# A small triangular solve on VectorE, and decays stored without their padding, in a recurrence kernel

## The chip, the cores and the metric

The kernel runs on one core of a Trainium2 chip. The metric is the device time of one execution in microseconds (us). Executions of one kernel scatter: eleven runs of the kernel before took 1129.26 to 1141.66 us in one set of rounds and 1132.16 to 1147.00 us in another. A kernel is always timed next to runs of the kernel before on the same chip, and compared with those; a ratio counts runs of the undisturbed (fast) state alone. In the profiles PE is TensorE, PEld its weight loads, DVE VectorE, ACT ScalarE, POOL GpSimd and SP SyncE; the granted clock is the share of TensorE's full clock that it was given.

## The reference

A recurrence over 768 time steps for 4 batches and 8 heads of 40 values, then a feed-forward layer over the 3,072 tokens:

```python
for t in range(S):                                   # S = 768; state: [B, H, 40, 40]
    y[:, :, t] = einsum('bhd,bhde->bhe', rt, state)
    Sa = einsum('bhde,bhe->bhd', state, at)
    state = state * wt[:, :, None, :] - einsum('bhd,bhe->bhde', Sa, bt)
    state = state + einsum('bhd,bhe->bhde', vt, kt)
x = y as [B*S, H*D]                                  # 3072 x 320
out = maximum(x @ w_in, 0)**2 @ w_out                # 320 -> 2048 -> 320
```

The kernel works on chunks of 128 steps: 24 chunks (6 in time for each of 4 batches, batch running fastest), so that the recurrence becomes matrix products and a triangular system per chunk and head. `rest` makes a chunk's products with k, v and r, `chain` carries the state through it, and the feed-forward layer is woven in once groups of chunks are done.

## The kernel before

Three parts matter. First, the preparation of a chunk (`early`): products of decays by scans, their reciprocals, and a' = a times decay, all in one tile `dec` of 128 partitions with 3 x 4 x 130 values. Heads sit in pairs: one in partitions 0 to 39, the other in 64 to 103; the rest is padding. For all chunks but the first two the tile is stored to DRAM and read back an iteration ahead of its use:

```python
    def load(i, g=None):
        x_ = loaded[i] = {"k": fetch("k", k, i)}
        if g is not None:
            g["dec"] = new("dec", [128, 3, NP, C + 2], 2)
            nc.sync.dma_start(out=g["dec"], in_=kept_e[i])
        x_["r"] = fetch("r", r, i)
        ...
    def early(i, g=None):
        dec = decays.next() if g is None else new("dec", [128, 3, NP, C + 2], 2)
        if g is not None:
            nc.vector.memset(dec[:, :A_, :, MID:MID + 1], 1.0)
        ...                      # scans, reciprocals, bT, a' on VectorE
        if g is None:
            store(kept_e[i], dec)
        ...                      # N = products of a' and bT, stored to kept_q or kept_d
```

Second, the triangular solve. N of one or more chunks (a "unit"; the first two units are one chunk each) is gathered from DRAM into `half_n`, solved by pairs of small operations on GpSimd, stored, and read back as `blocks`, from which T, the inverse, is joined:

```python
    def solve(u, between={}):
        ...
        for s in range(size - 1):
            if s in between:
                between[s]()
            ...
            nc.gpsimd.tensor_tensor(p_, part[...], t3[...], Alu.mult)
            nc.gpsimd.tensor_tensor(t3[:, :n, s + 1:], t3[:, :n, s + 1:], p_, Alu.subtract)
        nc.gpsimd.dma_start(out=to, in_=ts)
    def inverses(i, g, queue=nc.sync):
        blocks = new("blocks", [128, H, Q], 1)
        for col in range(classes(u)):
            queue.dma_start(out=blocks[col::classes(u)], in_=...)
        ...                      # transpose on VectorE, small products, T
```

Third, the order at the start. The program gives each engine a stream of operations in its own order; `go` advances a generator by a step. While GpSimd solves unit 0, VectorE prepares chunks 2 and 3 (`e2`, `e3`):

```python
    solve(0, {12: lambda: take(1, own)})      # take: fetch the next unit's N
    go(r0)
    load_early(3)
    go(r0, 4)
    go(e2, 2)
    load(1)
    go(first_slot)
    ...                                       # e2 and e3 to their ends
    join = inverses(0, ready[0])
    go(join)
    go(e3)
    flush()
    solve(1, {8: lambda: weights_by(0, nc.gpsimd), 20: lambda: take(2, own)})
    run(r0)
    run(join)
    weights_by(1, nc.sync)                    # 1 MB of weights on the SP queue
```

## Time and profile before

| | before |
|---|---|
| median of 3 runs (range) | 1133.54 us (1133.11 to 1136.49) |
| span of the profiled run, mean granted clock | 1135.1 us, 0.908 |
| first product with T on TensorE | 59.06 us |
| chunk 0's tokens on VectorE | 95.81 us |
| chunk 3's tokens | 226.55 us |
| last chunk's tokens | 1057.83 us |

The last four rows are the milestones. "Tokens" is the product of VectorE that ends a chunk. Each is read from one profiled run, so a few us can be chance: the kernel `fill_only` below ends 5.7 us late in its profile, taken in the slowest of its six runs, and has a ratio of 1.0008. In the timeline of the kernel before (start, duration, engine, line, operation, output and inputs, and in brackets the idle time ahead of it and what ended that) they are:

```profile
95.81 0.63 DVE L615 TENSOR_TENSOR tokens<-ps_c,dec 128x512 f32<-128x512 f32 x1
...
226.55 0.69 DVE L615 TENSOR_TENSOR tokens<-ps_c,dec 128x512 f32<-128x512 f32 x1 [3.04 <-PE ps_c L87]
...
1057.83 0.69 DVE L615 TENSOR_TENSOR tokens<-ps_c,dec 128x512 f32<-128x512 f32 x1 [1.96 <-PE ps_c L87]
```

The list of waits (engine, line and output that waited, what it waited for, us in total, times, longest) has four kinds of inputs for the kernel before, 13.0 us together:

```profile
PE ps_w L315 <- DMA in_w<-in_w_dram: 4.9, 2, 4.3
PE ps_w L315 <- DMA in_r<-in_r_dram: 4.3, 3, 2.7
PE ps_w L315 <- DMA in_v<-in_v_dram: 2.6, 2, 2.1
...
PE ps_w L315 <- DMA in_k<-in_k_dram: 1.2, 1, 1.2
```

### The profile page before, as it was taken

What the parts mean: (1) busy time and instruction counts of PE and PEld (TensorE: products, weight loads), DVE (VectorE), ACT (ScalarE), POOL (GpSimd) and SP (SyncE); (2) the same over time, 40 slices, a digit from 0 to 9 for tenths busy, and PEclk for the clock granted to TensorE, in tenths of its full rate; (3) what the DMA queues carried; (4) which work ended last, traced back from release to release, by engine and by line L of the source; (5) the groups of instructions that cost most, each with busy time, mean ns of one, the idle gap of its engine ahead of it and who ended that gap; (6) DMA issues with size and microseconds to landing.
All of it is one profiled execution on the core that took longest, in us unless ns stands there. A gap on an engine that the chain in (4) does not pass through costs nothing.

```text
span 1135.1 us, 19336 instructions
## 1 busy us (share of the span) xinstructions
PE 1029.9 (91%) x7632; PEld 811.9 (72%) x7632; DVE 482.1 (42%) x1004; ACT 246.2 (22%) x547; POOL 651.7 (57%) x1129
## 2 busy tenths in 40 slices
PE   6385787799999999999999999999999999999998
PEld 5375676668777777777777777777777777777666
DVE  6367877727355155154264253353143133330211
ACT  2123233222221122122112122113021121221111
POOL 5886628877874999603999802999858810000000
PEclk8666656689999999999989999999998999999999
DMA  9889977583648505519515518414243342030000
GB/s 116 154 151 210 182 177 178 124 154 77 135 106 156 121 36 109 152 39 167 116 48 101 123 65 150 118 49 84 58 117 69 77 90 58 10 83 12 7 12 12
DMA packets 262370, 113.48 MB, mean 100 GB/s; under 512 B 244168, under 2 KB 250440, under 8 KB 260616
## 3 DMA queue, kind: packets, MB, share of 16 engines
q1 hardware_dynamic: 257944, 93.24, 40.2%
q0 software_dynamic: 3248, 18.88, 7.0%
q8 instruction: 60, 0.98, 0.4%
q10 hardware_dynamic: 1088, 0.13, 0.2%
q14 instruction: 30, 0.25, 0.1%
HBM read 75.77 MB, written 34.48 MB: 97 GB/s over the span
## 4 chain that ended last, share of the span: by engine, by line
PE 69%; DVE 11%; DMA 10%; SPq 3%; POOL 2%; issue 2%; ACT 2%; DVEq 0%; POOLq 0%; ACTq 0%
PE ps_f L87 34%; PE ps_c L87 19%; PE ps_w L87 11%; PE ps_w L315 3%; DMA in_v<-in_v_dram 3%; DVE decay L358 1%; DVE decay L359 1%; PE ps_w L533 1%; SPq L108 1%; DMA in_r<-in_r_dram 1%; DMA blocks<-kept_t 1%; POOL half_t L435 1%; POOL half_p L433 1%; DMA in_w<-in_w_dram 1%; PE ps_c L543 1%
## 5 line engine op out<-in xcount | busy, mean ns | idle before, releaser
L433 POOL TENSOR_TENSOR half_p<-half_n,half_t 128x70 f32<-128x70 f32 (+52 forms) x502 | 288.5, 575 | 104.9 <-DMA half_n<-kept_d 55.4
L435 POOL TENSOR_TENSOR half_t<-half_t,half_p 128x70 f32<-128x70 f32 (+52 forms) x502 | 315.2, 628 | 39.3
L643 DVE TENSOR_TENSOR hid<-ps_f,hid 128x256 f32<-128x256 f32 x176 | 73.9, 420 | 350.3 <-ACT hid L642 349.9
L87 PE MATMUL ps_f<-w_out,hid 128*128 128x320 f32 x704 | 208.2, 444 | 0.1
L87 PE MATMUL ps_f<-tokens,w_in 128*128 128x256 f32 x704 | 199.5, 410 | 0.0
L87 PEld LDWEIGHTS ps_f<-w_out,hid 128*128 128x128 f32 x704 | 130.4, 193 | 49.5 <-issue 2.4
L87 PEld LDWEIGHTS ps_f<-tokens,w_in 128*128 128x128 f32 x704 | 124.6, 196 | 43.5 <-issue 30.3
L642 ACT ACTIVATE hid<-ps_f 128x256 f32<-128x256 f32 x176 | 67.4, 383 | 269.1 <-PE ps_f L87 268.6
L87 PE MATMUL ps_f<-tokens,w_third 64*128 64x256 f32 x352 | 86.0, 425 | 8.1 <-DVE hid L643 6.0
L87 PEld LDWEIGHTS ps_c<-xr,T 64*64 64x64 f32 x768 | 54.9, 150 | 23.6 <-issue 13.8
L87 PE MATMUL ps_c<-xr,T 64*64 64x40 f32 x768 | 60.7, 241 | 7.2 <-DMA T<-kept_t 2.4
L410 POOL DMA_DIRECT2D half_n<-kept_d x18 | 8.9, 501 | 98.0 <-DMA kept_d<-N 92.9
L87 PEld LDWEIGHTS ps_f<-tokens,w_third 64*128 64x128 f32 x352 | 40.0, 190 | 34.9 <-DVE hid L643 23.0
L354 DVE TENSOR_TENSOR_SCAN decay<-ps_w,ones 128x64 f32<-128x64 f32 x88 | 23.6, 268 | 85.1 <-PE ps_w L315 85.1
L87 PEld LDWEIGHTS ps_c<-in_v,A 128*128 128x128 f32 x384 | 51.2, 209 | 2.3
L87 PE MATMUL ps_c<-in_v,A 128*128 128x40 f32 x384 | 50.2, 294 | 0.0
L87 PE MATMUL ps_w<-rT,xnT 40*128 40x128 f32 x384 | 36.4, 309 | 12.6 <-DVE RV L331 12.1
L87 PEld LDWEIGHTS ps_w<-rT,xnT 40*128 40x128 f32 x384 | 29.9, 206 | 22.9 <-DVE RV L331 18.9
L615 DVE TENSOR_TENSOR tokens<-ps_c,dec 128x512 f32<-128x512 f32 x24 | 16.5, 688 | 66.1 <-PE ps_c L87 66.1
L545 ACT COPY sd<-ps_c 128x512 f32<-128x512 f32 x20 | 11.7, 586 | 144.8 <-PE ps_c L543 144.8
L87 PE MATMUL ps_w<-decay,bT 40*128 40x128 f32 x352 | 28.4, 307 | 14.6 <-DVE decay L363 14.6
L370 ACT COPY N<-ps_w 128x512 f32<-128x512 f32 x48 | 25.8, 589 | 63.8 <-PE ps_w L87 44.2
(148 smaller groups left out, 1441.8 us busy)
## 6 DMA issues: line engine op xcount, KB each, us to landing
kept_e<-decay SPq DMA_DIRECT2D x22, 780.0 KB
dec<-kept_e SPq DMA_DIRECT2D x22, 780.0 KB
half_n<-kept_d POOLq DMA_DIRECT2D x12, 384.0 KB, 9.4
half_n<-kept_d POOLq DMA_DIRECT2D x6, 768.0 KB, 11.5
in_w<-in_w_dram SPq DMA_DIRECT2D x24, 160.0 KB
in_ab<-in_b_dram SPq DMA_DIRECT2D x24, 160.0 KB
in_ab<-in_a_dram SPq DMA_DIRECT2D x24, 160.0 KB
in_k<-in_k_dram SPq DMA_DIRECT2D x24, 160.0 KB
```

The source lines that it names most:

```text
L87: nc.tensor.matmul(o, l_, r_, start=start, stop=True, skip_group_check=True)
L108: later(lambda: queue.dma_start(out=out_, in_=in_), steps)
L315: nc.tensor.transpose(p_[:, q * 128:(q + 1) * 128], pair(x_, q), ident)
L354: nc.vector.tensor_tensor_scan(up[:, q, MID + 1:C + 1], wT[:, q, MID:], ones, 1.0, Alu.mult, Alu.mult)
L358: nc.vector.reciprocal(down[:, :, MID + 1:C + 1], up[:, :, MID + 1:C + 1])
L370: nc.scalar.copy(t_[:, e * NP:(e + 1) * NP], p_)
L433: nc.gpsimd.tensor_tensor(p_, part[:, at:at + m_].unsqueeze(1).to_broadcast([128, n, m_]), t3[:, :n, s:s + 1].to_broadcast([128, n, m_]), ...
L435: nc.gpsimd.tensor_tensor(t3[:, :n, s + 1:], t3[:, :n, s + 1:], p_, Alu.subtract)
L545: nc.scalar.copy(sd.rearrange("p q e d -> p q (e d)"), quads(p_))
L615: nc.vector.tensor_tensor(t_, y_, g["up"][:, :, :C], Alu.mult)
L642: nc.scalar.activation(h_, p_, Act.Relu)
L643: nc.vector.tensor_tensor(h_, p_, h_, Alu.mult)
```

## The change

The intent has two parts. GpSimd's solve of the first unit is on the way to the first T, and VectorE was expected to do it faster; so this one solve goes to VectorE, with its input issued ahead and its products in PSUM, and its result goes to DRAM and back on ScalarE's queue. And the decays go without their padding: two transfers of 40 rows (243.75 KB each) instead of one of 128 (780 KB), for which the tiles must hold valid padding, so GpSimd fills them once at the start. The diff, cut to its core:

```diff
@@ load
-            g["dec"] = new("dec", [128, 3, NP, C + 2], 2)
-            nc.sync.dma_start(out=g["dec"], in_=kept_e[i])
+            g["dec"] = whole_decays.next()
+            for e, rows in enumerate(both):
+                nc.sync.dma_start(out=g["dec"][rows], in_=kept_e[i][e])
@@ rings
+    whole_decays = Ring("whole", 2, [128, 3, NP, C + 2], 1.0, lambda t_: t_[:, :A_])
+    for t_ in whole_decays.tiles:
+        nc.gpsimd.memset(t_[:, A_], 0.0)
+    both = [slice(e * DP, e * DP + D) for e in range(2)]
@@ early
-            store(kept_e[i], dec)
+            for e, rows in enumerate(both):
+                store(kept_e[i][e], dec[rows])
@@ solve
-    def solve(u, between={}):
+    def solve(u, between={}, engine=nc.gpsimd):
...
-        nc.gpsimd.dma_start(out=to, in_=ts)
+        (nc.gpsimd if engine is nc.gpsimd else nc.scalar).dma_start(out=to, in_=ts)
@@ the start
-    solve(0, {12: lambda: take(1, own)})
     go(r0)
     load_early(3)
-    go(r0, 4)
-    go(e2, 2)
     load(1)
+    flush()
+    solve(0, engine=nc.vector)
+    join = inverses(0, ready[0], nc.scalar)
+    go(join)
+    take(1, own)
+    go(r0, 2)
+    go(e2)
+    go(r0, 2)
     go(first_slot)
...                              (e2, e3 and join now follow here, step by step)
```

More of the change, by code (lines that the diff above doesn't have):

```diff
@@ L294 @@
     Q = HC // 2
-    kept_e = [dram.tile([128, 3, NP, C + 2], FP32, tag=f"e{i}", name=f"kept_e{i}") for i in range(len(order))]
+    kept_e = [dram.tile([2, D, 3, NP, C + 2], FP32, tag=f"e{i}", name=f"kept_e{i}") for i in range(len(order))]
     sizes = [1, 1] + [2] * 4 + [4] * ((len(order) - 12) // 4) + [2]
@@ L346, in early @@
         x_ = early_loaded.pop(i)
-        dec = decays.next() if g is None else new("dec", [128, 3, NP, C + 2], 2)
-        if g is not None:
-            nc.vector.memset(dec[:, :A_, :, MID:MID + 1], 1.0)
+        dec = decays.next() if g is None else whole_decays.next()
         up, down, aT = (dec[:, n] for n in (UP, DOWN, A_))
@@ L431, in solve @@
             at = s * size + s + 1 if s < Q else Q * HC + (s - Q) * (Q + 1) + 1
-            p_ = new("half_p", [128, 528], 1)[:, :n * m_].rearrange("p (j t) -> p j t", j=n)
-            nc.gpsimd.tensor_tensor(p_, part[:, at:at + m_].unsqueeze(1).to_broadcast([128, n, m_]),
+            p_ = new("half_p", [128, 528], 1) if engine is nc.gpsimd else psum(ps_f)
+            p_ = p_[:, :n * m_].rearrange("p (j t) -> p j t", j=n)
+            engine.tensor_tensor(p_, part[:, at:at + m_].unsqueeze(1).to_broadcast([128, n, m_]),
                                     t3[:, :n, s:s + 1].to_broadcast([128, n, m_]), Alu.mult)
-            nc.gpsimd.tensor_tensor(t3[:, :n, s + 1:], t3[:, :n, s + 1:], p_, Alu.subtract)
+            engine.tensor_tensor(t3[:, :n, s + 1:], t3[:, :n, s + 1:], p_, Alu.subtract)
         to = kept_t[u]
         to = to.rearrange("n b h f k j t -> (n b h f k) (j t)") if fine else to.rearrange("n b h f j t -> (n b h f) (j t)")
-        nc.gpsimd.dma_start(out=to, in_=ts)
+        (nc.gpsimd if engine is nc.gpsimd else nc.scalar).dma_start(out=to, in_=ts)
     def inverses(i, g, queue=nc.sync):
@@ L731 @@
     flush()
-    solve(0, {12: lambda: take(1, own)})
     go(r0)
     load_early(3)
-    go(r0, 4)
-    go(e2, 2)
     load(1)
-    go(first_slot)
-    go(e2, 2)
-    go(e3, 2)
+    flush()
[6 more added lines that the diff above has]
+    go(r0, 2)
+    go(first_slot)
+    go(e2)
+    go(join)
+    go(e2)
+    go(e3)
+    go(join)
+    go(e2)
+    go(e3)
+    go(join)
     go(e2)
@@ L743 @@
     flush()
-    join = inverses(0, ready[0])
-    go(join)
     go(e3)
     flush()
-    solve(1, {8: lambda: weights_by(0, nc.gpsimd), 20: lambda: take(2, own)})
+    solve(1, {14: lambda: weights_by(0, nc.gpsimd)})
+    take(2, own)
     run(r0)
```

## The prediction

> **What bounds the kernel now.** I read first the busy shares in 40 slices of the span (28.4 us each), then the busy time of each engine in stretches.
>
> ```profile
> PE   6385787799999999999999999999999999999998
> PEclk8666656689999999999989999999998999999999
> ```
>
> ```profile
> 0.00:40.00 40.00, 26.02 (x172) 22.41 (x174) 27.89 (x60) 8.74 (x16) 25.30 (x90) 0.83 1.04 129
> 40.00:80.00 40.00, 21.83 (x197) 20.14 (x196) 14.11 (x28) 8.35 (x17) 31.77 (x110) 0.54 0.68 146
> 80.00:120.00 40.00, 26.65 (x259) 23.88 (x259) 30.82 (x56) 12.50 (x24) 25.01 (x68) 0.63 1.00 198
> ...
> 400.00:600.00 200.00, 187.63 (x1392) 146.60 (x1391) 86.42 (x171) 39.05 (x87) 133.85 (x153) 0.95 0.42 95
> ```
>
> The columns of the second view are: stretch, its length, busy us (and count) of PE, PEld, DVE, ACT, POOL, then granted clock, DMA share, GB/s. There are two regimes. From about 240 us on TensorE is busy 94% and more, at nearly full clock, and the rest of the machine hides behind it: nothing saved there on VectorE, GpSimd or in a transfer shortens the run unless PE waits for it. Before 240 us PE is idle some 73 us in total (240 minus the 167.4 us of the six stretches up to there), at a clock of 0.54 to 0.66 after the first 40 us, and latencies decide. A gain or loss of this change must arise before 240 us and is then carried to the end one for one.
>
> So I followed the start in order of time. The lines that decide:
>
> ```profile
> 22.85 0.24 POOL L433 TENSOR_TENSOR half_p<-half_n,half_t 128x31 f32<-128x31 f32 x1 [3.14 <-issue]
> ...
> 47.42 0.61 POOL L438 DMA_DIRECT2D kept_t<-half_t  x1 [0.30 <-POOL half_t L435]
> ...
> 54.09 0.45 DVE L467 STREAM_TRANSPOSE hid<-blocks 128x256 f32<-128x256 f32 x1 [15.09 <-DMA blocks<-kept_t]
> ...
> 59.06 1.93 PE L87 MATMUL ps_c<-xr,T 64*64 64x40 f32 x16 [0.51 <-ACT T L486]
> ```
>
> ```profile
> 62.07 0.29 DVE L354 TENSOR_TENSOR_SCAN decay<-ps_w,ones 128x64 f32<-128x64 f32 x1 [7.53 <-PE ps_w L315]
> ...
> 88.90 0.45 DVE L467 STREAM_TRANSPOSE hid<-blocks 128x256 f32<-128x256 f32 x1 [4.44 <-DMA blocks<-kept_t]
> ```
>
> The first chunk's triangular solve runs on GpSimd from 22.85 to 47.4 us (62 small operations, and 2.5 us to start the next unit's input), its result goes through DRAM and is back at 54.1, the inverse T is joined and the chain starts at 59.1. VectorE sits idle for 15.1 and 7.5 us meanwhile, because chunks 2 and 3 were prepared (done by 39 us) in the shadow of the solve. Unit 1 is then solved until 74.8, and its blocks, landing at 88.9, hold VectorE once more, for 4.4 us only. Between 62 and 107 us VectorE is otherwise nearly always busy, so its in-order stream paces that stretch.
>
> [...]
> - [...] 685 ns for 128x512, 480 ns for 128x320[...].
> - [...] the 128x320 product of two SBUF tensors (L525) takes 597 ns, the 128x320 sum with one PSUM operand (L596) 491 ns.
> - [...] I counted the kernel's 579 transfers on the SP queue by their leading dimension (128, 64, 32 and 16 give 16, 24 gives 12, 40 gives 10, 8 gives 8); by this rule they must post 8,792 completions, and the trace has exactly 8,792 four-byte packets on that queue.
>
> ```profile
> L331 DVE TENSOR_TENSOR A<-ps_w,upper 128x512 f32<-128x512 f32 x48 | 30.9, 685 | 13.8 <-PE ps_w L87 13.8
> ...
> L525 DVE TENSOR_TENSOR state<-state,f 128x320 f32<-128x320 f32 x20 | 11.9, 597 | 0.7
> L537 DVE TENSOR_TENSOR in_k<-ps_w,in_k 128x320 f32<-128x320 f32 x24 | 11.5, 480 | 0.0
> L596 DVE TENSOR_TENSOR state<-ps_c,state 128x320 f32<-128x320 f32 x20 | 9.8, 491 | 23.6 <-PE ps_c L87 23.6
> ```
>
> **The change part by part.**
>
> *Transfers without padding.* 44 transfers of 780 KB (22 stores, 22 loads) become 88 of 243.75 KB: 12.9 MB of 113.5 MB less. [...] The records of the 6,240 B packets show bursts of 2.1 us where nothing else runs, which is 8 packets of some 0.24 us. What is left are 44 more issues on SP (0.35 to 0.6 us each, median, against 1,135 us) and one more slot in the ring of eight completion semaphores that SP's transfers wait on in turn: in a crowded stretch the queue blocks one transfer sooner. Together 0, at most a few us of loss.
>
> *The new ring.* The tiles for decays of chunks 0 and 1 are now filled by GpSimd before use, not marked by two VectorE memsets of 65 ns. GpSimd's stream has the two fills of the old ring (128x1560, 2.74 us together) first, then the new ones of 128x1040. Before, that point is reached at 8.40 us; one fill more, 1040/1560 of 1.34 us, is 0.9 us, so the first scan, which now waits for it, starts at 9.4 and not at 5.40 us: plus 4.0 us on the chain to the first solve, which should start at 26.7.
>
> *The solve on VectorE.* 31 pairs with 1,560 elements per operation kind, mean 50. [...] as each waits for the one before (the dependent pair L265, L266 starts 0.68 us apart at 0.65 us duration) about 0.23 us: 62 x 0.23 = 14.3 us against 22 on GpSimd. GpSimd starts unit 1 at about 35 us beside it[...]: end at about 42, against 47.4. The way through DRAM stays: 6.7 us (47.4 to 54.1).
>
> *What moves.* ScalarE now issues that way, and waits in it, before it copies rT and kvT; and VectorE, in order, can do chunk 0's second masks and all of chunks 2 and 3 only after the solve. After the end at 42: store and reload issues 4.5, the two copies 1.2, products 2, masks 1.3, scaling 0.9 (with a PE wait of 1), scans 1.5, transpose 0.45: 54.7. Then chunks 2 and 3: four reciprocals 6.6, four products 2.5, scans 1.5: 65.3. In the PE stream the first product with T stands behind chunk 3's products (2.1 us): about 67 us, against 59.1. So the solve is 5 us earlier and the chain starts 8 us later, since the work that lay in the shadow of GpSimd's solve now lies behind VectorE's.
>
> *What is won back.* Unit 1 is solved from 35 to about 60 us instead of 75, so the 4.4 us wait at 88.9 goes. Net at the end of the first iteration: +8 - 4.4 = +3.6 us. Nothing later turns on unit 1.
>
> **The rivals.** (a) The early solve does carry through: if a VectorE operation costs 0.15 us instead of 0.23 and the shadow work fits into the 7 us of the way through DRAM, the chain starts at about 52 and 7 us or more are won, some 1,122 with the wait at 88.9. For it speak VectorE's 22 idle us before 62 us; against it, its in-order stream, in which the masks wait for ScalarE. (b) The bytes count after all: the stretch from 80 to 120 us has a DMA share of 1.00, and landings of 9 us (the kept_e store at 98.5) are on the chain of waits. If the transfers were bound by the sum over engines, 1.5 us per crowded transfer on some 8 of them would give 5 to 12 us: 1,122 to 1,128. [...] (d) The ring of eight semaphores delays the input loads that PE waits for later (in_v and in_r take 14 to 15 us three times on the chain): 2 to 4 us more.
>
> **Range and chances.** The sum says 1,133.5 + 3.6 = 1,137. Rivals (a) and (b) are together likelier than (c) and (d), so I take 3 off: 1,134 us, with 1,119 to 1,148 for 8 in 10. 2% is 22.7 us, more than any single rival gives; faster 0.05, same 0.90, slower 0.05.
>
> **What would show it.** First scan near 9.4 us and the solve on VectorE from 26.7 to 42: ring and operation cost right. First product with T near 67 us: order right; near 52: rival (a). Bursts of the decays still over 2 us in quiet stretches[...]: transfer part right. PE busy from 240 us unchanged. The prediction is wrong if the chain starts before 55 us and that lead is kept to 240 us, or if PE's waits for in_v and in_r after 240 us shrink or grow.

The sum came to 1,133.5 + 3.6 = 1,137 us, and to 1,134 with 3 taken off for the rivals. Four of its terms or their reasons are cut: the 0.20 us that, with some 0.03 us of wait, made the 0.23 us of one operation; 1 us of contention, with which the solve ends at 42 (26.7 + 14.3 + 1); the reason for giving the transfers no time; and rival (c), 9 us more. A straight line through the two measured means (685 ns for 512 elements, 480 ns for 320) gives 138 ns plus 1.07 ns per element, so 0.19 us for 50 and 13.7 us instead of 14.3 for the 62 with the same wait (an estimate from these two means); the solve took 15.6 us.

## The result and the profile after

The changed kernel took 1160.93 us in the median of 4 runs (1158.56 to 1163.38), the kernel before in the same rounds 1134.75 us (1133.11 to 1136.49, 4 runs). A ratio here is always the mean time of one kernel's fast runs over the mean of the other's of the same rounds, so not quite the ratio of the medians; it is 1.0231, with a 95% interval of 1.0201 to 1.0260. The change made the kernel slower by 2.3%, and the prediction (1,134 us, at most 1,148) was wrong. The profiled run spans 1158.1 us, 23.0 more than the one before.

The two slices of the page that the prediction began with, and the stretches of the windows view (stretch, length, busy us and count of PE, PEld, DVE, ACT, POOL, then clock, DMA share, GB/s), now for the changed kernel:

```profile
PE   5375786979999899999999999999999999999998
...
PEclk9996555569999899899999899999999999999999
```

```profile
0.00:40.00 40.00, 15.02 (x84) 12.13 (x84) 25.25 (x83) 6.08 (x11) 16.91 (x59) 1.00 0.91 112
40.00:80.00 40.00, 27.64 (x216) 25.29 (x217) 23.61 (x53) 8.83 (x19) 21.79 (x72) 1.00 0.51 98
80.00:120.00 40.00, 25.42 (x244) 23.46 (x243) 25.11 (x47) 10.22 (x21) 23.69 (x64) 0.71 0.90 143
...
400.00:600.00 200.00, 191.51 (x1409) 149.11 (x1408) 76.02 (x162) 39.06 (x87) 133.99 (x155) 0.97 0.49 89
```

In the first 40 us TensorE does 15 us of work where it did 26, since the preparation of chunks 2 and 3 has moved behind the solve. From 400 to 600 us it is as full as before (191.5 of 200 us against 187.6). So the loss lies at the start, as the prediction said any difference would. The milestones show it step by step:

```profile
109.78 0.63 DVE L621 TENSOR_TENSOR tokens<-ps_c,whole 128x512 f32<-128x512 f32 x1
...
250.40 0.69 DVE L621 TENSOR_TENSOR tokens<-ps_c,whole 128x512 f32<-128x512 f32 x1 [3.04 <-PE ps_c L87]
...
1080.59 0.69 DVE L621 TENSOR_TENSOR tokens<-ps_c,whole 128x512 f32<-128x512 f32 x1 [1.96 <-PE ps_c L87]
```

Chunk 0 ends 14.0 us later than before, chunk 3 23.8 us, the last chunk 22.8. More than half is lost before the first chunk is out, the rest in the next three, and from 250 us on hardly anything moves. Now the first hundred microseconds in order of time, over several engines (ACTq is ScalarE's queue, SPq that of SyncE):

```profile
9.40 0.29 DVE L358 TENSOR_TENSOR_SCAN whole<-ps_w,ones 128x64 f32<-128x64 f32 x1 [8.37 <-POOL whole L121]
...
26.78 0.20 DVE L439 TENSOR_TENSOR ps_f<-half_n,half_t 128x31 f32<-128x31 f32 x1 [0.42 <-issue]
...
42.16 0.17 DVE L441 TENSOR_TENSOR half_t<-half_t,ps_f 128x8 f32<-128x8 f32 x1
...
42.41 0.35 ACTq L444 DMA_DIRECT2D kept_t<-half_t  x1
44.16 2.65 ACTq L461 DMA_DIRECT2D blocks<-kept_t  x4
46.85 0.59 ACT L520 COPY rT<-ps_w 128x512 f32<-128x512 f32 x1 [21.00 <-DMA blocks<-kept_t]
...
50.08 1.29 DVE L337 TENSOR_TENSOR RV<-ps_w,upper 128x512 f32<-128x512 f32 x2 [7.75 <-PE ps_w L87]
...
69.77 1.92 PE L87 MATMUL ps_c<-xr,T 64*64 64x40 f32 x16
...
77.57 1.73 SPq L254 DMA_DIRECT2D w_out<-in_moe_w_in_dram  x4
79.40 0.65 SPq L142 DMA_DIRECT2D in_w<-in_w_dram  x1
...
92.51 1.09 PE L321 MATMUL ps_w<-ident,in_w 128*128 128x128 f32 x4 [8.03 <-DMA in_w<-in_w_dram]
...
96.97 0.49 DVE L602 TENSOR_TENSOR state<-ps_c,state 128x320 f32<-128x320 f32 x1 [10.60 <-PE ps_c L87]
...
102.87 0.43 DVE L473 STREAM_TRANSPOSE hid<-blocks 128x256 f32<-128x256 f32 x1
```

Up to the end of the solve everything stands where the prediction put it: first scan 9.4, solve 26.8 to 42.3. Then ScalarE, whose queue carries the way through DRAM, comes to its copies of rT and kvT only at 46.85, and VectorE idles 7.75 us for what depends on them; this too was in the prediction's sum (it puts the masks at 49.7; they start at 50.08). The first product with T starts at 69.77 (predicted 67, before 59.06). New is what follows. The SP queue had nothing to issue from 38 to 51 us, then chunk 4's inputs and from 59 us on the stores of chunks 2 and 3, which before were out by 56. The second block of weights was issued at 56.35 before and now at 77.57, and the w of chunk 5 stands right behind it: issued at 79.40, landed 13 us later, with TensorE idle 8.03 us for it and VectorE, behind TensorE, 10.60 us. In the kernel before, VectorE waited 4.02 us at that place:

```profile
79.35 0.49 DVE L596 TENSOR_TENSOR state<-ps_c,state 128x320 f32<-128x320 f32 x1 [4.02 <-PE ps_c L87]
```

The wait of 4.4 us for unit 1's blocks (at 88.90 before) is gone: VectorE takes them at 102.87 without idling. But the new wait ahead of it is larger than what this saved, and it is why VectorE comes after the blocks, which landed at 100.1.

The input waits of TensorE have grown from 13.0 to 27.4 us:

```profile
PE ps_w L321 <- DMA in_w<-in_w_dram: 13.4, 3, 8.0
PE ps_w L321 <- DMA in_r<-in_r_dram: 8.1, 4, 4.3
PE ps_w L321 <- DMA in_k<-in_k_dram: 5.9, 3, 3.8
```

Finally the transfers themselves, from the packet records of the two traces. I call the 6,240-byte packets of one chunk's store or reload a burst, and take its time from first start to last end. Before: 128 packets, shortest burst 2.06 us, median 2.86, median packet 239 ns. After: 80 packets, shortest 3.08, median 3.55, median packet 296 ns. Five eighths of the bytes take longer. (The count of completions in the prediction held. On the SP queue of the kernel before, the landing records show 16 per transfer for 128, 64, 32 and 16 rows, and 13, 11 and 9 for 24, 40 and 8; these three are one more than the prediction's list, which fits the four-byte packets. With 44 transfers of 16 gone, 88 of 10 come, and four reloads of 16 gone to ScalarE's queue, the list makes 8,792 - 704 + 880 - 64 = 8,904 four-byte packets on the SP queue, and the trace has 8,904. In the twelve shortest bursts of each trace, 14.7 to 15.0 packets were in flight on the mean before and 7.0 to 9.4 after. Which engine took which packet the records do not tell.)

### The profile page after: what moved, and what is told of

Same layout as the page of the kernel before. It is cut to its first block, busy times and chain, and to the rows that moved or that the text cites. A ratio compares the mean times of both kernels' runs of the same rounds, so it can differ in the third digit from the quotient of the medians.

```text
span 1158.1 us, 19364 instructions
## 1 busy us (share of the span) xinstructions
PE 1043.3 (90%) x7632; PEld 824.2 (71%) x7632; DVE 494.4 (43%) x1064; ACT 246.3 (21%) x547; POOL 638.2 (55%) x1070
## 4 chain that ended last, share of the span: by engine, by line
PE 72%; DVE 11%; DMA 10%; SPq 2%; ACT 2%; issue 2%; POOL 1%; ACTq 0%; DVEq 0%; POOLq 0%
PE ps_f L87 34%; PE ps_c L87 19%; PE ps_w L87 12%; PE ps_w L321 4%; DMA in_r<-in_r_dram 4%; DVE decay L362 1%; PE ps_w L539 1%; DVE decay L363 1%; DMA blocks<-kept_t 1%; DMA whole<-kept_e 1%; DMA in_w<-in_w_dram 1%; SPq L108 1%; DVE RX L337 1%; PE ps_c L549 1%; DVE hid L649 1%
## 5 line engine op out<-in xcount | busy, mean ns | idle before, releaser
L439 POOL TENSOR_TENSOR half_p<-half_n,half_t 128x252 f32<-128x252 f32 (+47 forms) x471 | 281.4, 598 | 119.9 <-DMA half_n<-kept_d 58.1
L441 POOL TENSOR_TENSOR half_t<-half_t,half_p 128x252 f32<-128x252 f32 (+47 forms) x471 | 306.8, 651 | 36.9
L87 PE MATMUL ps_w<-rT,kvT 40*128 40x128 f32 x384 | 29.8, 298 | 21.9 <-ACT kvT L522 21.9
L87 PE MATMUL ps_w<-rT,xnT 40*128 40x128 f32 x384 | 36.7, 312 | 10.9 <-DVE RV L337 10.2
L87 PEld LDWEIGHTS ps_w<-rT,kvT 40*128 40x128 f32 x384 | 25.1, 200 | 29.6 <-ACT kvT L522 25.9
L621 DVE TENSOR_TENSOR tokens<-ps_c,whole 128x512 f32<-128x512 f32 x24 | 16.5, 689 | 68.8 <-PE ps_c L87 68.8
```

The source lines that it names most:

```text
L87: nc.tensor.matmul(o, l_, r_, start=start, stop=True, skip_group_check=True)
L439: engine.tensor_tensor(p_, part[:, at:at + m_].unsqueeze(1).to_broadcast([128, n, m_]), t3[:, :n, s:s + 1].to_broadcast([128, n, m_]), Alu ...
L441: engine.tensor_tensor(t3[:, :n, s + 1:], t3[:, :n, s + 1:], p_, Alu.subtract)
L621: nc.vector.tensor_tensor(t_, y_, g["up"][:, :, :C], Alu.mult)
```

## The experiments

Theory after the result: both parts cost. (1) The solve costs by order: ScalarE's queue, then the late transfer queue. (2) The transfers cost although they move fewer bytes. The rivals were that one of the two parts is innocent, or that the fills of the new ring are behind it. 18 kernels ran; all were correct but one. Two of the correct ones had a mistake, told below. "Base" names the kernel that a diff starts from.

### Each part alone

`solve_only`, base after: one padded transfer and the old tiles again, no fills.

```diff
-            for e, rows in enumerate(both):
-                nc.sync.dma_start(out=g["dec"][rows], in_=kept_e[i][e])
+            nc.sync.dma_start(out=g["dec"], in_=kept_e[i])
```

> The first chunk is solved on VectorE in the changed order, but the decays travel as before (one padded transfer of 780 KB, tiles without the GpSimd fill). Theory 1 (both parts cost): the chain starts some 4 us earlier than in the changed kernel, near 66 us against 59 before, the inputs of chunk 5 still stand behind weights on the SP queue, so about 10 us slower than before, 1,142 to 1,147 us. Theory 2 (all of the loss is the order of the start): about 1,155 to 1,160 us. Theory 3 (all of it is the transfers): 1,131 to 1,136 us.

`moves_only`, base before: two halves of 40 rows in two fixed tiles that are not filled (one column is set by VectorE, as before). Where a diff shows a reload in another shape, as here, the store has the same shape.

```diff
-            g["dec"] = new("dec", [128, 3, NP, C + 2], 2)
-            nc.sync.dma_start(out=g["dec"], in_=kept_e[i])
+            g["dec"] = whole_decays.next()
+            for e, rows in enumerate(both):
+                nc.sync.dma_start(out=g["dec"][rows], in_=kept_e[i][e])
```

> The kernel before with the decays stored and loaded in two halves of 40 rows, and no fill by GpSimd; the solve stays on GpSimd. Theory 1: the start is as before (first product with T near 59 us), and each of the first four iterations loses some 3 us, so 8 to 14 us slower than before, 1,143 to 1,149 us; bursts of the 6,240 B packets near 3.4 us against 2.1 in quiet stretches. Theory 2: 1,133 to 1,137 us. Theory 3: 1,155 to 1,162 us.

`after_nofill`, base after: the ring's tiles are not filled by GpSimd.

> The changed kernel without the GpSimd fills of the new ring (two VectorE memsets as before). If the fill's 4 us at the start go through to the end: 1,156 to 1,158 us, first scan at 5.4 us. If they are absorbed later by waits for transfers: 1,160 to 1,162 us.

`after_48`, base after: halves of 48 rows, not 40.

```diff
-    both = [slice(e * DP, e * DP + D) for e in range(2)]
+    both = [slice(e * DP, e * DP + 48) for e in range(2)]
```

> The changed kernel with halves of 48 rows instead of 40: more bytes (585 instead of 487.5 KB each way), [...] If the few engines make the transfers slow: quiet bursts of about 2 us instead of 3.4, and 1,148 to 1,156 us. If it is the number of transfers and their slots on the SP queue, or the bytes: 1,160 to 1,164 us.

(Its first theory took 48 rows to be shared by more engines than 40; that was the author's estimate, no record shows it, and the clause is cut, as are the clauses on numbers of DMA engines in later expectations.)

Measured, 3 rounds, before 1133.68 us:

| run | us (range) | ratio [95%] | first T | chunk 0 | chunk 2 |
|---|---|---|---|---|---|
| after (its own rounds) | 1160.93 (1158.56 to 1163.38) | 1.0231 [1.0201, 1.0260] | 69.77 | +14.0 | +21.0 |
| solve_only | 1148.58 (1144.41 to 1151.67) | 1.0117 [1.0060, 1.0175] | 64.78 | +10.9 | +12.1 |
| moves_only | 1146.50 (1145.76 to 1148.83) | 1.0115 [1.0069, 1.0161] | 58.62 | -3.0 | +4.1 |
| after_nofill | 1152.87 (1147.65 to 1156.39) | 1.0164 [1.0110, 1.0218] | 64.45 | +11.3 | +13.7 |
| after_48 | 1160.55 (1152.97 to 1161.36) | 1.0220 [1.0165, 1.0275] | 69.95 | +14.5 | +16.8 |

("First T" is the start of the first product with T in the profiled run; the chunks are milestones minus those of before.) Neither part is innocent: 1.2% each. Their patterns differ: the solve's loss is there with chunk 0 (+11.2 us at chunk 3, +14.9 at the end, with +20 on the way), the transfers' loss builds up from chunk to chunk (+6.5 us at chunk 3, +9.6 at the end). The parts do not simply add. after_nofill holds both without the fills, and took less than both expectations for it (1,156 us or more): 1.0164, where 1.0117 x 1.0115 would make 1.0233. And in this order the fills do cost something: with them the first T comes 5.3 us later (69.77 against 64.45) and the ratio is 1.0231 against 1.0164, though the two intervals overlap.

In moves_only the loss shows as TensorE's waits for inputs, 21.9 us against 13.0:

```profile
PE ps_w L325 <- DMA in_k<-in_k_dram: 6.6, 3, 4.5
PE ps_w L325 <- DMA in_v<-in_v_dram: 5.6, 3, 4.6
PE ps_w L325 <- DMA in_w<-in_w_dram: 5.2, 2, 4.2
PE ps_w L325 <- DMA in_r<-in_r_dram: 4.5, 3, 1.9
```

So the halved transfers pay less in their own wait (VectorE waited 3.9 us for them, 1.2 before) than in the inputs queued behind them (8.9 us more). And halves of 48 rows instead of 40 (after_48) cured nothing: the bursts stayed at 3.0 us and over, and the time at 1160.55 us. Whether they ran on more engines is not shown.

### Why two smaller transfers are dearer: place in the queue, or rows

Two suspicions were left. Heads in partitions 0 to 39 and 64 to 103 mean that each of the two transfers touches one half of the partitions only, and packets to one half may be slower: the median was 296 ns in the changed kernel against 239 before. That the half is the reason was a guess at this point. The other suspicion was the number of transfers in SP's queue, which issues one after the other (none of its 579 issues in the kernel before overlaps the next).

`two_ranges` and `two_combs`, base before: two transfers of 64 rows into the old rotating tiles, same bytes, same 6,240-byte packets; only the rows differ.

```diff
-            nc.sync.dma_start(out=g["dec"], in_=kept_e[i])
+            for e, rows in enumerate(both):
+                nc.sync.dma_start(out=g["dec"][rows], in_=kept_e[i][e])
+    both = [slice(e * 64, (e + 1) * 64) for e in range(2)]      # two_ranges
+    both = [slice(e, 128, 2) for e in range(2)]                 # two_combs
```

> The kernel before, with the 780 KB of decays and a' sent as two transfers of 64 rows, rows 0 to 63 and rows 64 to 127: same bytes, same 6,240-byte packets[...]. Theory 1 (a transfer that touches only one half of the partitions is slow): bursts of both halves 3.3 to 3.8 us where nothing else runs, against 2.1 for the single transfer, and the time close to the run of halves of 40 rows (1,146.5), so 1,144 to 1,152. Theory 2 (the cost comes of more transfers: issues, slots of the completion ring, more wait edges): also 1,143 to 1,150, but bursts near 2.1 to 2.6 us. Theory 3 (few engines or the ring of tiles cost it): 1,131 to 1,137.

> The same as the run before it, but the two transfers take the even and the odd rows, so each of them touches all of the partition range. [...] Theory 1 (half of the partitions): bursts 2.1 to 2.5 us and 1,131 to 1,138 us. Theory 2 (number of transfers): 1,143 to 1,150, the same as with two ranges. Theory 3: 1,131 to 1,137, as with two ranges.

| run | us (range) | ratio [95%] | shortest burst | median packet |
|---|---|---|---|---|
| two_ranges | 1159.42 (1154.08 to 1167.30) | 1.0210 [1.0171, 1.0250] | 3.50 us | 439 ns |
| two_combs | 1154.80 (1151.86 to 1164.02) | 1.0179 [1.0137, 1.0221] | 2.04 us | 240 ns |
| before | 1136.04 (1129.26 to 1141.66) | | 2.06 us | 239 ns |

The bursts settle the speed of the packets: 64 rows of one half take 439 ns a packet, 64 rows out of all partitions 240, with everything else equal. But the time does not follow. The combs, whose packets are as fast as before, lost 19 us all the same, and the two intervals overlap: between these two runs the slow packets cost nothing that can be told. Both times lie above every range that I had given. My theory of the half of the partitions alone fell. What the combs lose shows in the waits:

```profile
DVE kvT L507 <- DMA dec<-kept_e: 25.2, 5, 6.7
...
PE ps_w L87 <- DVE kvT L507: 22.7, 6, 5.8
```

VectorE waited 25.2 us for the reloaded decays (before: 1.2 us), five times, TensorE 22.7 us behind it. One of these places, first in the kernel before, then with the combs (timeline of the SP queue; the second number is how long an issue took, waits inside it included):

```profile
341.47 0.80 SPq L152 DMA_DIRECT2D dec<-kept_e  x1
342.31 0.43 SPq L142 DMA_DIRECT2D in_r<-in_r_dram  x1
342.79 0.58 SPq L142 DMA_DIRECT2D in_v<-in_v_dram  x1
343.47 3.55 SPq L142 DMA_DIRECT2D in_b<-in_b_dram  x1
347.06 8.74 SPq L142 DMA_DIRECT2D in_w<-in_w_dram  x1
```

```profile
347.29 1.28 SPq L153 DMA_DIRECT2D dec<-kept_e  x2
348.62 0.77 SPq L142 DMA_DIRECT2D in_r<-in_r_dram  x1
349.43 3.37 SPq L142 DMA_DIRECT2D in_v<-in_v_dram  x1
352.90 8.15 SPq L142 DMA_DIRECT2D in_b<-in_b_dram  x1
...
360.54 0.69 DVE L507 TENSOR_TENSOR kvT<-ps_w,dec 128x512 f32<-128x512 f32 x1 [6.23 <-DMA dec<-kept_e]
```

The two long issues, some 3.5 and 8.5 us, hit in_b and in_w before and in_v and in_b with the combs: exactly one transfer earlier. I took this for the ring of eight completion semaphores with one transfer more in the round, but that is not shown. The trace of the kernel before does show eight semaphores on SP's transfers, each used 72 or 73 times, nearly always by every eighth transfer (560 of 575), and no issue that ended before the transfer ahead of it on its semaphore had landed (none of 575). But at these two issues that transfer had landed before they began (at 340.5 us for in_b, 342.0 for in_w): in_b's wait ended with TensorE (346.0), and what held in_w's the trace does not tell. And the second comb landed late: issued by 348.6 us, 63 of its 64 packets ran from 353.6 to 358.6 us at a median of 464 ns, and its last completion came at 360.4. They ran next to 12 KB packets of GpSimd's queue, which start at 350.0, while before all 128 packets were through by 346.7, when those of GpSimd's queue had just begun (346.3). So part of the delay may be this meeting, and not the queue.

`rows_104`, base before: one transfer again, of rows 0 to 103, in two fixed tiles.

```diff
-            g["dec"] = new("dec", [128, 3, NP, C + 2], 2)
-            nc.sync.dma_start(out=g["dec"], in_=kept_e[i])
+            g["dec"] = whole_decays.next()
+            nc.sync.dma_start(out=g["dec"][both], in_=kept_e[i])
+    both = slice(0, DP + D)                                     # 104 rows
```

> The kernel before with its decays and a' sent as one transfer of rows 0 to 103 (634 KB instead of 780[...]), into two fixed tiles. Theory 1 (the second transfer costs the time: it stands one place further back in the in-order SP queue and its ring, and comes late at the start of an iteration): no second transfer, so the time of the kernel before, ratio 0.995 to 1.004, VectorE's waits for the decays in total under 4 us (the two combs: 25 us). Theory 2 (the fixed tiles, or any departure from 128 rows, cost it): ratio 1.008 to 1.015 as in the run of the transfers alone.

1152.28 us (1151.38 to 1157.20), ratio 1.0136 [1.0114, 1.0159]. This refutes the theory of the second transfer as the only cause: a single transfer with 19% fewer bytes loses as much. Its packets took 399 ns in the median and its shortest burst 3.18 us, and TensorE's waits for inputs grew to 22.7 us. Why its packets are slower than those of 128 rows (239 ns) no run shows.

`moves_act` (base moves_only) and `combs_act` (base two_combs): the second reload is issued on ScalarE's queue; the stores stay on SP's.

```diff
-                nc.sync.dma_start(out=g["dec"][rows], in_=kept_e[i][e])
+                (nc.scalar if e else nc.sync).dma_start(out=g["dec"][rows], in_=kept_e[i][e])
```

> The run of the transfers alone (two halves of 40 rows in the kernel before, ratio 1.0115), with the second half's reload issued on ScalarE's queue instead of SP's. Theory 1 (order and ring of the SP queue): the reloads no longer lengthen that queue, and over half of the 12.8 us goes: ratio 0.999 to 1.006. Theory 2 (the DMA engines or the memory side are the limit, whoever issues): ratio 1.008 to 1.016 as before, since the same packets move.

> The two combs (even and odd rows, ratio 1.0179), with the second comb's reload on ScalarE's queue. Bursts of 2.1 us for a reload stay. Theory 1 (the second transfer costs by its place in SP's in-order queue and ring): two thirds or more of the 18 to 20 us go, ratio 0.999 to 1.006, and VectorE's wait for the decays falls from 25 us to under 8. Theory 2 (two transfers instead of one cost it whoever issues them): ratio 1.012 to 1.020, and VectorE's wait stays above 15 us.

moves_act: 1144.70 us (1137.37 to 1149.82), ratio 1.0059 [1.0027, 1.0091] instead of 1.0115. combs_act: 1148.33 us (1142.60 to 1153.72), ratio 1.0101 [1.0061, 1.0141] instead of 1.0179; VectorE's 25.2 us of waits for the decays are gone from its list. So for the combs, whose two intervals barely overlap, the place in SP's queue is a good part of the cost. For the halves it is likely, but not shown: their two intervals overlap more widely, and the runs are of different rounds. Not two thirds of the loss came back; the cure has a wait of its own, and whether that is all of the rest is not shown. In the first iteration ScalarE idles 8.7 us around that issue, and TensorE waits for the copy that ScalarE makes after it (combs_act, timeline of PE):

```profile
111.10 1.92 PE L87 MATMUL ps_c<-xr,T 64*64 64x40 f32 x16 [8.65 <-ACT xr L570]
```

`narrow_128`, base before: one transfer of all 128 rows, 975 of 1,560 columns, the bytes of the two halves. The result is wrong (relative error 0.124).

```diff
+    sent = lambda t_: t_.rearrange("p n q c -> p (n q c)")[:, :975]
-            g["dec"] = new("dec", [128, 3, NP, C + 2], 2)
-            nc.sync.dma_start(out=g["dec"], in_=kept_e[i])
+            g["dec"] = whole_decays.next()
+            nc.sync.dma_start(out=sent(g["dec"]), in_=kept_e[i])
```

> The kernel before with one transfer of all 128 rows but only the first 975 of the 1,560 columns (487.5 KB, the bytes of the two halves of 40 rows); the rest of the tile keeps old values, so chunks from 4 on compute with partly wrong decays on purpose. Theory 1 (bytes are worth little; only a full-width single transfer is free of loss): bursts of 1.2 to 1.4 us, ratio 0.990 to 1.000. Theory 2 (bytes do bind the crowded stretches): 44 transfers by 0.8 us, most of it gained: ratio 0.975 to 0.988. Theory 3 (any departure from the tuned schedule loses a per cent, such as the fixed tiles): ratio 1.006 to 1.015.

1130.49 us (1125.85 to 1136.69), ratio 0.9949 [0.9911, 0.9987], shortest burst 1.35 us. This is what the saved bytes are worth with full-width packets and one transfer: half a per cent. Fixed tiles in place of rotating ones are in this run too, so they cost no more than the bytes gain; fill_only below, with all bytes and fixed tiles, agrees (1.0008). Against this run, rows_104 differs in its rows and bytes alone.

### The solve's part: which order costs

`sp_trip`, base solve_only: the way of the first T through DRAM on SP's queue, which is idle then (in the changed kernel it issued nothing from 38 to 51 us).

```diff
-        (nc.gpsimd if engine is nc.gpsimd else nc.scalar).dma_start(out=to, in_=ts)
+        (nc.gpsimd if engine is nc.gpsimd else nc.sync).dma_start(out=to, in_=ts)
-    join = inverses(0, ready[0], nc.scalar)
+    join = inverses(0, ready[0])
```

> The part with VectorE's solve alone, old single transfers, no new ring, and the way of the first T through DRAM issued on the SP queue instead of ScalarE's. Theory 1 (ScalarE, which waits in that way before it copies rT and vT, holds VectorE for some 7 us): those copies come right after the solve, VectorE's second masks by 43 us instead of 46 to 50, the first product with T 3 to 7 us earlier than in the run with the solve alone (64.8), and 1,141 to 1,146 us. Theory 2 (VectorE's order, which puts chunks 2 and 3 behind the solve, costs all of it): the copies come earlier, but the first product with T and the time stay within 2 us of the run with the solve alone (1,148.6).

1139.87 us (1136.56 to 1143.72), ratio 1.0034 [0.9999, 1.0068], against 1.0117 for solve_only: ScalarE's queue was the larger part of the loss (the rounds are different ones, and the intervals overlap slightly). VectorE's second masks follow the solve at 37.0 us with no wait, and the first product with T starts at 55.43, 9.3 us earlier than in solve_only and 3.6 earlier than in the kernel before. Still chunk 0 ends 1.2 us later than before. The wait for chunk 5's w is there again, and long:

```profile
79.73 1.08 PE L316 MATMUL ps_w<-ident,in_w 128*128 128x128 f32 x4 [8.01 <-DMA in_w<-in_w_dram]
```

`sp_trip_w`, base sp_trip: `weights_by(1, nc.sync)` moved from its place after the join to just before `solve(0, engine=nc.vector)`.

> The run before it, with the second block of weights fetched on the SP queue before the solve, where that queue has nothing to do, instead of after the join, where the inputs of chunk 5 queue behind it. Theory 1 (the transfer queue that fell behind costs a good part: in_w of chunk 5 lands 13 us after its issue and PE waits 8 us): PE's wait for in_w near 90 us goes, and 3 to 8 us are won against the run before it. Theory 2 (VectorE's stream alone sets the pace there): within 2 us of the run before it.

1139.99 us (1125.73 to 1146.38; the last one counts as slow and is not in the ratio), ratio 1.0002 [0.9954, 1.0049]: not clearly different from sp_trip. The wait for in_w was gone, but the weights now held up the first T: its blocks were issued at 44.88 instead of 38.88 us, and the first product with T came at 62.14. Inconclusive by itself, but it says where the weights belong: behind the blocks.

`early_w` and `early_w_chain` put them there, the second with several steps of the first chain ahead of the preparation.

```diff
     go(first_slot)
+    load_early(4)
+    weights_by(1, nc.sync)
     go(e2)
...
-    weights_by(1, nc.sync)
```

> The run of the solve on VectorE with its way through DRAM on the SP queue (ratio 1.0034), with the second block of weights issued right after the blocks' reload and the inputs of chunk 4, so behind the first T and before chunk 5's inputs. In the run where the weights stood before the solve, PE's wait of 8.0 us for in_w was gone but the blocks landed 5.8 us later. Theory 1 (the late transfer queue is what is left of the loss): both at once, first product with T at 55 to 57 us, no wait of PE for in_w over 3 us before 100 us, chunk 0's tokens 3 to 8 us earlier than in the kernel before, ratio 0.992 to 1.000. Theory 2 (VectorE's stream sets the pace from 60 us on): first product at 55 to 57 but chunk 0's tokens within 2 us of the kernel before, ratio 1.000 to 1.004.

> The run before it, with the first chain's products with T and N put into TensorE's stream as soon as T is joined, ahead of the preparation of chunks 2 and 3. Theory 1 (PE's order holds the chain once T is early): first product with T at 49 to 51 us, chunk 0's tokens another 4 to 6 us earlier, ratio 0.988 to 0.998. Theory 2 (what follows is bound by VectorE's stream and GpSimd's second solve): first product at 49 to 51, but the time within 2 us of the run before it.

They took 1130.43 us (1123.45 to 1137.97), ratio 0.9930 [0.9894, 0.9966], and 1138.97 us (1130.69 to 1144.78), ratio 1.0004 [0.9970, 1.0038]. But both have a mistake. The inputs a and b rotate over four tiles, two per chunk; chunk 4's were fetched in program order before chunk 2 had read its own from the same two tiles. So chunk 2 was prepared with chunk 4's a and b. The error stayed within the tolerance, as a and b are small here (0.05), so the runs count as correct, which they are not. The trace gave it away, as TensorE waited 16.1 us for a transfer that chunk 2 has no business with:

```profile
47.92 1.09 PE L316 MATMUL ps_w<-ident,in_ab 128*128 128x128 f32 x4 [16.11 <-DMA in_ab<-in_b_dram]
```

`weights_mid` repeats the test with chunk 4's inputs where the kernel had them, and the weights right behind; `weights_mid_t` adds the first product with T ahead of the rest of chunks 2 and 3.

```diff
     go(e2)
     go(e3)
+    weights_by(1, nc.sync)
     go(join)
     go(e2)
     go(e3)
     go(join)
+    go(first_slot)                  # weights_mid_t only
...
-    weights_by(1, nc.sync)
```

> The run of the solve on VectorE with its way through DRAM on SP's queue (ratio 1.0034), with the second block of weights issued after the blocks' reload and after chunk 4's inputs, which are fetched where the kernel fetched them before (once chunk 2's a and b are read). Theory 1 (the late transfer queue is what is left of the loss): first product with T at 54 to 57 us, PE's 8.0 us wait for in_w gone, chunk 0's tokens 3 to 8 us earlier than in the kernel before, ratio 0.988 to 0.997. Theory 2 (VectorE's stream sets the pace): in_w's wait gone but chunk 0's tokens within 2 us of the kernel before, ratio 0.998 to 1.004.

> The run before it, with the first product with T put into TensorE's stream right after the join, ahead of the products and transposes of chunks 2 and 3. Theory 1 (PE's order holds the chain): first product with T at 48 to 51 us and a ratio 0.002 to 0.006 lower than that run. Theory 2 (what follows is set by VectorE's stream and GpSimd's second solve): first product at 48 to 51, ratio within 0.002 of that run, or higher, since the preparation of chunk 3 and its stores come later.

weights_mid: 1131.55 us (1122.58 to 1134.22), ratio 0.9942 [0.9904, 0.9980]. The solve's part is now a small gain. TensorE's wait for in_w fell to under 2 us and was one for VectorE, not for the transfer, and chunks 0 and 3 end 3.1 and 3.8 us earlier than in the kernel before, the last one 5.0:

```profile
92.68 0.63 DVE L617 TENSOR_TENSOR tokens<-ps_c,dec 128x512 f32<-128x512 f32 x1
...
222.73 0.69 DVE L617 TENSOR_TENSOR tokens<-ps_c,dec 128x512 f32<-128x512 f32 x1 [2.67 <-PE ps_c L87]
...
1052.84 0.69 DVE L617 TENSOR_TENSOR tokens<-ps_c,dec 128x512 f32<-128x512 f32 x1 [1.96 <-PE ps_c L87]
```

weights_mid_t: 1131.83 us (1127.87 to 1138.86), ratio 0.9969 [0.9928, 1.0009]. The first product with T starts at 50.08 us, 7.3 earlier, chunk 0 ends 8.2 us earlier than before, chunk 1 only 1.2: the lead of the chain does not last. That was the second theory.

### The fills, and the sum

`fill_only`, base before: the changed kernel's ring with its fills, one transfer as before. `after_mended`, base after: the two mended orders of weights_mid, fills and halves left in.

> The kernel before with the changed kernel's ring of filled tiles for the decays (two fills of 128x1040 and two of 128x520 on GpSimd), still sent as one transfer of 128 rows. Theory 1 (the first scan waits for one fill more and the lead is lost on the chain to the first T and nowhere else): first scan near 9.3 us instead of 5.4, first product with T 3 to 4.5 us later, ratio 1.002 to 1.005. Theory 2 (the fills also hold GpSimd's first solve and what follows, or the fixed tiles cost something later): ratio 1.006 to 1.010.

> The changed kernel with its two order faults mended as in the run weights_mid (way of the first T through DRAM on SP's queue, second block of weights behind the blocks' reload), transfers in halves and fills left in. If the terms add (order 1.0117 to 0.9942, transfers 1.0115, fills 1.003 to 1.007): ratio 1.008 to 1.014. If the halves' cost came mostly from being late together with the late queue (terms that do not add): 0.998 to 1.006.

fill_only: 1137.12 us (1133.73 to 1142.52), ratio 1.0008 [0.9966, 1.0050]. The first scan waits until 9.40 us, as predicted, and the first product with T comes at 62.69 us, 3.6 later; in the time no loss can be told from none.

after_mended: 1142.24 us (1140.65 to 1148.23), ratio 1.0058 [1.0019, 1.0097]. Two moved issues take back three quarters of the changed kernel's loss (1.0231 to 1.0058). What is left is near what the terms measured alone give (0.9942 x 1.0115 x 1.0008 = 1.0064), but it falls in the range that I had given for terms that do not add (0.998 to 1.006), and the interval covers both. With after_nofill above, whose two parts cost less together than their product, I take the sum as a rough guide and not as shown.

No version that I ran and that computes the right thing beats weights_mid. It beats the kernel before by 0.6% and the changed kernel by some 29 us (1160.93 against 1131.55, in different rounds). Full-width transfers and the mended order are what it has.

## Why the prediction was wrong, step by step

**What bounds the kernel: right for this change.** The difference arose before 250 us (23.8 us at chunk 3) and was carried to the end (22.8 us). It is no rule for the transfers: the combs were 5.1 us late at chunk 3 and 19.4 at the end, rows_104 7.4 and 17.5. The clock is a rival that I did not test: from 120 to 240 us TensorE was granted 0.50 to 0.54 in the changed kernel's profile and 0.63 to 0.66 before. fill_only had 0.54, 0.54 and 0.63 there at a ratio of 1.0008, so little of the 2.3% is likely to come of it.

**The ring: right.** First scan at 9.40, predicted 9.4. By itself it is worth 3.6 us at the first T and nothing that can be told at the end; in the changed kernel's order 5.3 us at the first T (after_nofill).

**The solve on VectorE: right.** 26.78 to 42.33 us, predicted 26.7 to 42; the first operations came 0.22 to 0.31 us apart (0.23 in the estimate). The 597 ns that the prediction shows for L525 is a mean: sixteen of its twenty took 491 to 494 ns, and the other four, 662 to 1,267 ns, all ran beside GpSimd, as ten of the sixteen did. So the contention for which the prediction added 1 us is not shown by it.

**What moves: right in kind, a little small.** First product with T at 69.77, predicted 67. The 2.8 us between them are mostly a wait that the sum left out: VectorE idles 2.29 us for TensorE at 66.07. The prediction had ScalarE's wait in its sum, but took it as given; sp_trip shows that this one choice of queue was worth 0.8%.

**What is won back: this step failed.** It said that "the 4.4 us wait at 88.9 goes" and "+8 - 4.4 = +3.6 us". Measured at chunk 0: +14.0. The 4.4 us did go, but the step followed VectorE's stream and left out the queue that the moved work feeds. Behind the solve, the weights were issued 21 us later (56.35 to 77.57), and chunk 5's w, right behind them, came 13 us after its issue: TensorE waited 8.03 us, and VectorE 10.60 where it had waited 4.02. So the stretch from the first product with T to chunk 0's tokens changed by +3.3 us (14.0 - 10.7) instead of -4.4: 4.4 won, 6.6 lost at this wait and 0.9 at one behind it make 3.1 of it. weights_mid, which moves that one issue, shows it: the stretch took 35.3 us, against 41.6 in sp_trip and 36.8 before, and the ratio was 0.9942 against 1.0034. And the 4.4 us went for another reason than predicted. Unit 1 was solved earlier (by 64.4 instead of 74.8 us), but its blocks were read back only at 91.35, as their issue stood behind the same inputs; they landed at 100.1, and without the 7.5 us of new waits VectorE would have stood some 4.7 us for them (an estimate: 102.87 - 7.5 = 95.4). In weights_mid they landed at 78.3 and were taken at 85.77.

**Transfers without padding: this step failed too.** The prediction gave this part no time, from an estimate of rows per DMA engine that no trace shows. Its count of completions was right (8,904 packets) and beside the point. Bursts went from 2.06 to 3.08 us at their shortest, and the part alone cost 1.15%. Two things are shown: packets to rows of one half of the partitions were slow here (439 against 240 ns), and two transfers in place of one cost 1.8% even with fast packets (combs: 25.2 us of waits for the decays). That slow packets alone cost time is shown by rows_104 only (399 ns, one transfer, 1.4%), and why its packets are slow is open. two_ranges, with both faults, is not clearly slower than the combs, and moves_only, with both and fewer bytes, cost 1.15%. So the costs do not add, and how that 1.15% splits stays open. (The bytes saved were 13.2 MB by the packet records, not 12.9.) The "one more slot in the ring" that the prediction named, "at most a few us", was the right place, the SP queue, with the wrong size; that the ring is the cause is not shown.

**The rivals.** (a), an early chain, did not come up in this order; when it did (weights_mid_t, 50.08 us), the lead was gone by chunk 1. (b), bytes, is worth 0.5% where it can act. (c), contention of VectorE with GpSimd, was hardly tested: GpSimd started its own next solve only at 39.96 us (35 in the prediction), when VectorE's was nearly done; the last products beside it took 0.18 to 0.26 us. (d), delayed inputs, was named with 2 to 4 us for in_v and in_r and was right in kind: TensorE's input waits grew by 14.4 us, but 8.03 of them are chunk 5's w, which the weights held up and not the ring. Of the signs named at the end, TensorE's waits for in_v and in_r after 240 us went from 6.2 to 7.4 us, and its busy time from 240 to 1130 us from 860.7 to 856.3.

## What to carry to other kernels

Moving work to an idle engine also moves every transfer that the work feeds (here the weights, by 21 us); follow the in-order queues as closely as the engines, and ask of each issue what now stands behind it. In this kernel the reload was best as one transfer over all 128 partitions: cutting columns gained 0.5% (in a run that computes wrongly), while cutting rows or splitting it in two lost 1.2 to 2.1%. And an engine that has copies to make should not carry a queue whose transfers wait on another engine, as ScalarE did here for 0.8%.
